# An mLSTM with a Fourier mixing block on one Trainium2 core: the second batch folded twice with named PSUM banks, a weight piece and the later recurrences moved by three slots

## The chip, the core and the metric

The kernel runs on one core of a Trainium2 chip. A core has a matrix engine (PE, with its weight loads listed apart as PEld), a vector engine (DVE), an activation engine (ACT), a general engine (POOL) and a queue that issues transfers (SP). Each runs its own instructions strictly in the order in which they were written; semaphores make one wait for another. SBUF is the working memory of all of them; PE writes its results to PSUM, which is divided into banks, and the others read them there. The metric is the time of one execution in microseconds (us), less being better. The time before is the median of three runs.

## What is computed

All of it is float32; the two weights arrive as float64 and are converted on the chip. First an mLSTM cell runs over 768 steps for 4 batches of 8 heads of width 40; its output, 768 rows of 320 per batch, goes through a Fourier mixing block with a normalization and a two-layer MLP of hidden width 1280:

```python
# mLSTM, per batch and head, for t in range(768):
m_new = np.maximum(f_gate[:, :, t] + m, i_gate[:, :, t])
f_stab = np.exp(f_gate[:, :, t] + m - m_new)
i_stab = np.exp(i_gate[:, :, t] - m_new)
C = f_stab * C + i_stab * outer(vt, kt)
n = f_stab * n + i_stab * kt
y[:, :, t] = sigmoid(o_gate[:, :, t]) * (C @ qt) / np.maximum(np.abs(n @ qt), 1.0)
...
# fnet block on x of (4, 768, 320)
mixed = np.real(np.fft.fft(np.fft.fft(x, axis=1), axis=2))
u = x + mixed
un = (u - mean(u)) / np.sqrt(var(u) + 1e-06)
out = u + np.maximum(un @ w_ch1, 0.0) @ w_ch2
```

## The kernel before

**Tiles and stages.** A batch has six chunks of 128 rows. The code counts batches from 0, so "batch 2" of the change's title is `b == 1`; below they are called by their index. Each batch runs through four stages:

- the recurrence, chunk by chunk and in halves of 64 rows (helper at L547): `ps` holds scores and the state's products, `ph` the outputs, `C0` to `C2` the state; `mlstm_mask`, `halves_decay` on POOL, `halves_add` (L703) and `halves_weigh` (L708) on DVE. `mlstm_finish` (L741 to L759) divides and multiplies by the gate, and writes the chunk into `x`;
- folding and the Fourier transform over rows: `mix_fold` (L828 to L846) adds and subtracts mirrored chunks and columns into `fe`; `mix_seq` and `mix_tail` multiply `fe` with the table `ds_sb` into `pz`, `pz` and `pzt`. For batches 2 and 3 `mix_fold_again` (L860, L862) first folds once more, and `mix_products_again` (L903) then needs narrower products than `mix_products` (L912 to L915), which batches 0 and 1 use;
- the transform over columns: `mix_feat` (L946) gives `pu`, one for each pair of chunks; `mix_add` (L968 to L974) adds each chunk's part of it to `x` on DVE and takes the row statistics; `mix_center` subtracts the mean on ACT into `uc`; `mix_turn` (L989) transposes `uc` on PE into `put`; `mix_turn_out` (L994) copies that to `uT` on ACT. For the middle pair (chunks 1 and 4) two short DVE instructions, L963 and L964, stand ahead of chunk 4's additions;
- the MLP: `pm` (L1058, L1067, L1129, L1134), relu into the hidden tiles, `po` (L1192 in `mlp_out` for batch 0, L1248 in `mlp_out_pair` for the others, which also need sums of hidden tiles on DVE, L1234), `residual` (L1198) and a store.

Chunks of these stages are taken in the order 0, 5, 1, 4, 2, 3 (`ORDER`).

**What sets the order.** The whole program is a plan written out by hand. `at(slot, phase, fn, ...)` puts a call into a slot (0 to about 150) and a phase in it; `run` goes through the plan in sorted order and issues every call there and then. The phases are `EVAC, FILL, MAIN, FILL_PE = range(4)`, with fractions between them. So a slot number is a place in the order, not a time, and each engine gets its instructions in this one order. In most slots `MAIN` is one step of some batch's MLP on PE, while another batch's recurrence and mixing are fitted in around it. In the profiled execution slot 51 begins at 117.75 us, slot 63 at 171.4, slot 83 at 209.9, slot 95 at 259.9 and slot 115 at 298.6.

**Batches beside each other.** `plan_batch(b, s_mlstm, s_mix, s_mlp)` starts the recurrence, the mixing and the MLP of a batch. The mixing and the last recurrence of batch 1 fall into the output stage of batch 0's MLP (slots 51 to 62: twelve half blocks of five `po` matmuls each, half by half for six blocks of rows); the recurrence of batch 2 begins in the same slots.

**Banks.** `bank(name, shape, n)` (L93) gives a PSUM tile in one of four banks, `pm0` to `pm3`. With a number it takes that bank; without one the next digit of a long string, `turn`. A tile that takes a bank waits until whatever was last in the bank has been read. Batches 2 and 3 take the numbers from the table `MIX` (L819): `pu` in banks 3, 2, 2 and `put` in 3, 3, 3, 3, 2, 3; batches 0 and 1 take them from the string.

**Weights.** Ten pieces are loaded as float64 and converted: `take` (L436, L438, DVE), `convert` (ACT), `join` (L450, L452, L456, DVE). Their slots are in the list `when`. The last piece, number 9, is the last part of the second weight.

Of the kernel before, what the change touches and what calls it, by code (L numbers as in the profile page):

```python
# [19 lines left out]
L = 128  # L20
# [37 lines left out]
def kernel(  # L58
# [723 lines left out]
    def plan_halves(b, s0, stride=3):  # L782
        at(s0 - 2, FILL + 0.7, halves_start, b)
        for c in range(NT):
            s = s0 + stride * c
            end = c == NT - 1
            t = 22 + 2 * c if b == 1 and c < 3 else s - 6
            at(t, FILL, mlstm_load, b, c)
            at(t, FILL, mlstm_load_max, b, c)
            at(t + 1 if c < 2 or b > 1 else s - 5, FILL, mlstm_load_decay, b, c)  # L790
            at(s - 2, FILL, mlstm_load_o, b, c)
            at(s - 2, FILL + 0.1, mlstm_scale_q, b, c)
            at(s - 2, FILL + 0.15, halves_alone, b, c)
            at(s - 1, FILL, mlstm_scale_v, b, c)
            at(s - 1, FILL, mlstm_exp, b, c, 0)
            at(s - 1, FILL + 0.5, mlstm_exp, b, c, NP)
            at(s, FILL, mlstm_mask, b, c)
            at(s, FILL_PE + 2.05, halves_scores, b, c)
            at(s, FILL_PE + 2.5, halves_to_state, b, c)
            for i in range(2):  # L800
                at(s + i, FILL + 0.05, halves_decay, b, c, i)
                at(s + 1 + i, FILL - 0.2, halves_add, b, c, i)
            at(s + 1, FILL, halves_weigh, b, c)
            at(s + 3, MAIN - 0.1 if end else FILL_PE, halves_from_state, b, c)
            at(s + 3, MAIN if end else FILL_PE + 0.5, halves_between, b, c)
            at(s + 3, FILL_PE + 3, halves_from_chunk, b, c)
            at(s + 3, FILL_PE + 0.6, mlstm_tanh, b, c)
            at(s + 4 + int((b, c) in ((2, 2), (3, 1))), FILL + 0.05, mlstm_finish, b, c)

# [4 lines left out]

    mixes = {}

    MIX = {"z": (2, 3), "zt": 2, "u": (3, 2, 2), "ut": (3, 3, 3, 3, 2, 3)}  # L819

    def copy(eng, out, in_):
        (nc.scalar.copy if eng == 0 else nc.vector.tensor_copy)(out=out, in_=in_)
# [41 lines left out]
    def mix_seq(b, p, parts):  # L864


        k = mixes.setdefault(b, Mix())
        if p == TG - 1:
            k.pz = getattr(k, "pz", []) + [bank("pz", [L, NK], MIX["z"][i] if b > 1 else None) for i in parts]
        for i in parts:  # L870
            if b < 2:
                mix_products(p, k.pz[i], i, slice(0, L))
            else:
                for product in mix_products_again(k, k.pz[i], i, slice(0, L)):
                    product()

    def mix_tail(b, p):

        k = mixes[b]
        if p == TG - 1:  # L880
            k.pzt = bank("pzt", [L, NK], MIX["zt"] if b > 1 else None)
        halves = [k.pzt[i * 64:(i + 1) * 64] for i in range(2)]
        if b < 2:
            for i in range(2):
                mix_products(p, halves[i], i, slice(L, PAD))
        else:

            a, z = (mix_products_again(k, halves[i], i, slice(L, PAD)) for i in range(2))
            for product in (a[0], z[0], a[1], z[1], a[2], z[2], a[3]):
                product()  # L890
# [37 lines left out]
    def mix_feat(b, p):  # L928

        k = mixes[b]
        m = slice(COL[p], COL[p] + L)
        pu = k.pu[p] = bank("pu", [L, DM + 1 + NC], MIX["u"][p] if b > 1 else None)
        if b == 0:
            products = ((pu[:, 0:DM + 1], k.Z[:, 0, m], dd_sb[:, 0]), (pu[:, 0:DM + 1], k.Z[:, 1, m], dd_sb[:, 1]),
                        (pu[:, 0:DM + 1], k.Zt[:, m], dd_sb[:, 2]))
        else:
            products = ((pu[:, 0:NC], k.Z[:, 0, m], dd_sb[:, 0, 0:NC]), (pu[:, NC:DM], k.Z[:, 1, m], dd_sb[:, 1, 1:HALF_D]),  # L940
                        (pu[:, 0:DM], k.Zt[:, m], dd_sb[:, 3, 0:DM]))
        if p == TG - 2:
            last, own = slice(LAST, LAST + 1), pu[0:1, DM + 1:]
            products += ((own, k.Z[:, 0, last], dd_sb[:, 0, 0:NC]), (own, k.Zt[:, last], dd_sb[:, 3, 0:NC]))
        for i, (o, z, t) in enumerate(products):
            nc.tensor.matmul(o, z, t, start=(i == 0), stop=(i in (2, 4)), skip_group_check=True)  # L946
# [37 lines left out]
    def mix_turn(b, c):  # L984

        k = mixes[b]
        pt = k.pt[c] = bank("put", [L, 3, L], MIX["ut"][ORDER.index(c)] if b > 1 else None)
        for ch in range(3):
            nc.tensor.transpose(pt[:, ch, :], k.uc[c].rearrange("p two n -> p (two n)")[:, ch * L:(ch + 1) * L], ident)  # L989

# [27 lines left out]
    def plan_mix(b, s0, x_done, s_feat, s_add, s_turn):  # L1018
        for j in range(TG):
            p = TG - 1 - j  # L1020
            at(x_done[j] + (b > 1 and j == TG - 1), FILL + 0.5 if b < 2 else FILL_PE + 0.2, mix_fold, b, p)
            if b == 0:
                at((s0 - 4, s0 - 2, s0)[j], FILL_PE + 4, mix_seq, b, p, (0, 1))
                at((s0 - 2, s0 - 2, s0)[j], FILL_PE + 4, mix_tail, b, p)
            elif b == 1 or j == 0:
                if b > 1:
                    for step, slot in enumerate((x_done[-1] + 2, x_done[-1] + 6)):
                        at(slot, FILL_PE + 0.25, mix_fold_again, b, step)
                at(s0, FILL_PE + 4, mix_seq, b, p, (0,))
                at(s0 + 1, FILL_PE + 4, mix_seq, b, p, (1,))  # L1030
                at(s0 + 2, FILL_PE + 4, mix_tail, b, p)
# [153 lines left out]
        nc.scalar.activation(out=h, in_=h, func=AF.Relu, scale=-1.0)  # L1185

    def mlp_out(b, gr, i, half):
        k = mixes[b]
        if half == 0:
            k.po = bank("po", [L, DM])  # L1190
        for f in range(half * NFF // 2, (half + 1) * NFF // 2):
            nc.tensor.matmul(k.po, hidden(gr, f)[:, i * L:(i + 1) * L], w2_sb[:, f, :], start=(f == 0), stop=(f == NFF - 1))  # L1192

    def residual(b, c, cols, po):

# [6 lines left out]

    def mlp_store(b, gr, i):
        c = ORDER[gr * TG + i]
        residual(b, c, slice(0, DM), mixes[b].po)
        store(b, c)


# [70 lines left out]
    def plan_mlp(b, s):  # L1279
# [27 lines left out]
        for gr in groups if b == 0 else ():  # L1307
            for i in range(TG):
                for half in range(2):
                    at(s, MAIN, mlp_out, b, gr, i, half)  # L1310
                    s += 1
                at(s, EVAC, mlp_store, b, gr, i)

    ctx.enter_context(tc.manual_schedule())
    eo_p = pool("eo", 1)
# [31 lines left out]
    s_mlp = 31  # L1347
    plan_batch(0, 0, 22, s_mlp)
    plan_batch(1, 32, 54, s_mlp + MLP_SLOTS)
    plan_batch(2, 51, 83, s_mlp + 2 * MLP_SLOTS)  # L1350
    plan_batch(3, 83, 115, s_mlp + 3 * MLP_SLOTS)
    for n in range(4):
        at(s_mlp + 2 * NFF + 1 + n, FILL + 0.4, weight_sums, n)
        at((56, 57, 58, 75)[n], FILL + 0.4, out_weight_sums, n)

    when = [((2, 0.7), (4, 0.5), (6, 0.6)), ((6, 0.7), (7, 0.5), (8, 0.6)), ((11, 0.7), (13, 0.5), (22, 0.6))]
    when += [((22, 0.7), (23, 0.7), (27, 0.6)), ((27, 0.7), (28, 0.7), (32, 0.6))]
    when += [((33, 0.7), (35, 0.7), (36, 0.6))] + [((s, 0.7), (s + 1, 0.7), (s + 2, 0.6)) for s in (36, 39, 42, 45)]
    pieces = w1_pieces + w2_pieces
    for n, (w, p) in enumerate(zip(when, pieces)):  # L1360
        if n > 4:
# [155 lines left out]
```

## Time and profile before

| | before |
|---|---|
| time, median of 3 runs | 404.14 us (402.89 to 404.44) |
| the profiled execution | 404.67 us |
| its span, first to last instruction | 402.9 us |
| mean granted clock of PE | 0.991 |
| PE busy | 387.8 us, 96% of the span |
| DVE busy | 279.8 us, 69% |
| ACT busy | 178.5 us, 44% |
| POOL busy | 128.0 us, 32% |

The span is what the trace covers; the profiled execution's time holds 1.8 us more. Two rows of the page show the span in 40 slices of 10.07 us, one digit per slice: PE's busy share in tenths, and the clock that was granted to PE in tenths of full speed:

```
PE   8999999999969999999999998999999999999996
PEclk9999999999989999999999999999999999999999
```

A 9 is 90% or more. The slice from 110.8 us has a 6 in the first row and an 8 in the second, the slice from 80.6 us an 8 in the second, and the slice from 241.8 us an 8 in the first; the first and the last slice hold the start and the end. The lines with the most idle time ahead of them on PE, from the page's costliest groups (line, engine, operation, out<-in with shapes, count | busy us, mean ns of one | idle before, and what ended most of it):

```
L1248 PE MATMUL po<-T,S 128*128 128x160 f32 x180 | 28.1, 303 | 2.6 <-DVE x L1198 2.6
L1129 PE MATMUL pm<-uT,w_sb 128*128 128x384 f32 x90 | 37.8, 507 | 0.2 <-DVE uT L1117 0.2
```

A float32 matmul is recorded as two instructions in the trace; five `po` matmuls of 128x320 appear as ten records and take 2.69 us when nothing interrupts them. Matmul ends are modelled, so a group's last row can overlap the next one's start by some tenths.

### The profile page before, as it was taken

Reading aid. Unit: us, or ns where it says so; the run is one execution under the profiler, and the core shown is the slowest. Engines: PE = TensorE matmul, PEld = TensorE weight load, DVE = VectorE, ACT = ScalarE, POOL = GpSimd, SP = SyncE. Lnnn points to the kernel's source line nnn. Section 1 sums busy time; section 2 is a strip of 40 time slices with the busy share of each in tenths; the row PEclk is TensorE's granted clock in tenths of the full one; section 3 lists DMA queues with packets and bytes.
Section 4 is the critical chain, followed back from the end, with each engine's and each line's share of the span. In section 5 each row is a group of like instructions: output and inputs, shape, how many; then the busy total and the mean of one; then the engine's idle time right before and its main releaser. Section 6 shows DMA issues by size and latency. Waiting matters only on the chain.

```text
span 402.9 us, 10837 instructions
## 1 busy us (share of the span) xinstructions
PE 387.8 (96%) x4324; PEld 283.3 (70%) x4324; DVE 279.8 (69%) x668; ACT 178.5 (44%) x513; POOL 128.0 (32%) x231
## 2 busy tenths in 40 slices
PE   8999999999969999999999998999999999999996
PEld 6887555556546776856569887855579997556996
DVE  7789976898867519787665689777663795336652
ACT  6898867576530213553562214544440023454000
POOL 5744425466945412261145304351200000020000
PEclk9999999989989999999999999999999999999999
DMA  7979499677752424365100525300000000000000
GB/s 197 278 227 320 121 240 257 194 242 240 191 151 70 142 87 131 109 196 150 54 26 2 157 82 170 103 20 2 1 0 18 17 34 33 2 0 0 34 34 34
DMA packets 22766, 43.96 MB, mean 109 GB/s; under 512 B 3492, under 2 KB 11388, under 8 KB 22588
## 3 DMA queue, kind: packets, MB, share of 16 engines
q1 hardware_dynamic: 22716, 43.27, 36.0%
q8 instruction: 34, 0.56, 0.5%
q14 instruction: 16, 0.13, 0.1%
HBM read 39.16 MB, written 4.10 MB: 107 GB/s over the span
## 4 chain that ended last, share of the span: by engine, by line
PE 80%; DVE 13%; issue 2%; POOL 2%; ACT 2%; DMA 0%; DVEq 0%; SPq 0%; POOLq 0%; ACTq 0%
PE po L1248 20%; PE pm L1129 16%; PE po L1192 8%; PE pm L1134 6%; PE ph L547 5%; PE ps L547 4%; PE pu L946 4%; PE pm L1067 4%; PE put L989 2%; PE pz L903 1%; PE pz L915 1%; DVE so L756 1%; PE pM L230 1%; PE pm L1058 1%; DVE x L759 1%
## 5 line engine op out<-in xcount | busy, mean ns | idle before, releaser
L1138 DVE TENSOR_TENSOR h<-h,pm 128x384 f32<-128x384 f32 x60 | 30.7, 550 | 30.6 <-PE pm L1129 16.5
L1198 DVE SCALAR_TENSOR_TENSOR x<-po,rstd,x 128x160 f32<-128x160 f32 (+1 forms) x69 | 27.0, 394 | 35.0 <-PE po L1248 32.3
L1129 PE MATMUL pm<-uT,w_sb 128*128 128x384 f32 x90 | 37.8, 507 | 0.2 <-DVE uT L1117 0.2
L543 POOL TENSOR_SCALAR_AFFINE_SELECT W<-W 64x512 f32<-64x512 f32 x36 | 27.9, 775 | 31.5 <-ACT W L518 30.4
L696 POOL TENSOR_TENSOR C<-C,decB 128x164 f32<-128x164 f32 x33 | 17.4, 528 | 62.1 <-DVE C L703 58.4
L518 ACT ACTIVATE W<-W,colT 128x64 f32<-128x64 f32 x144 | 36.5, 338 | 0.0
L1192 PE MATMUL po<-w_sb,h 128*128 128x320 f32 x120 | 35.2, 444 | 0.0
L1013 POOL TENSOR_TENSOR t<-rstd 128x6 f32<-128x6 f32 x12 | 2.6, 216 | 90.1 <-DVE v L1007 89.7
L1248 PE MATMUL po<-T,S 128*128 128x160 f32 x180 | 28.1, 303 | 2.6 <-DVE x L1198 2.6
L528 POOL TENSOR_TENSOR qg<-qk,Gb 128x512 f32<-128x512 f32 x21 | 27.3, 1298 | 9.5 <-DMA Gb<-G_d 9.5
L1192 PEld LDWEIGHTS po<-w_sb,h 128*128 128x128 f32 x120 | 22.7, 194 | 10.0 <-issue 1.5
L1067 PE MATMUL pm<-uT,w_sb 128*128 128x384 f32 x80 | 29.5, 505 | 0.1
L1248 PEld LDWEIGHTS po<-T,S 128*128 128x128 f32 x180 | 25.3, 190 | 4.5 <-DVE x L1198 3.4
L1248 PE MATMUL po<-w_sb,h 128*128 128x160 f32 x180 | 26.3, 300 | 0.0
L1248 PEld LDWEIGHTS po<-w_sb,h 128*128 128x128 f32 x180 | 25.2, 190 | 1.5 <-DVE x L1198 0.3
L994 ACT COPY uT<-put 128x384 f32<-128x384 f32 x24 | 11.1, 478 | 32.7 <-PE put L989 32.6
L1134 PE MATMUL pm<-uT,w1t_sb 64*128 64x384 f32 x120 | 25.2, 510 | 0.2 <-DVE h L1138 0.2
L1129 PEld LDWEIGHTS pm<-uT,w_sb 128*128 128x128 f32 x90 | 15.4, 189 | 14.0 <-DVE h L1138 4.9
L1185 ACT ACTIVATE h<-h 128x384 f32<-128x384 f32 x45 | 23.1, 520 | 2.0 <-DVE h L1138 2.0
L982 ACT ACTIVATE uc<-x 128x384 f32<-128x384 f32 x24 | 14.5, 614 | 18.9 <-DVE x L974 18.9
L703 DVE TENSOR_TENSOR C<-C,ps 128x164 f32<-128x164 f32 x33 | 10.5, 317 | 16.2 <-PE ps L547 13.6
L1067 PEld LDWEIGHTS pm<-uT,w_sb 128*128 128x128 f32 x80 | 14.5, 194 | 9.7 <-issue 1.4
(240 smaller groups left out, 860.8 us busy)
## 6 DMA issues: line engine op xcount, KB each, us to landing
kvt<-in_kv SPq DMA_DIRECT2D x24, 336.0 KB
qk<-in_qkT SPq DMA_DIRECT2D x48, 160.0 KB
raw<-in_w SPq DMA_DIRECT2D x10, 640.0 KB
Gb<-G_d SPq DMA_DIRECT2D x42, 128.0 KB
W<-M_d SPq DMA_DIRECT2D x36, 128.0 KB
so<-in_o SPq DMA_DIRECT2D x24, 160.0 KB
out<-x SPq DMA_DIRECT2D x24, 160.0 KB
ds_sb<-in_dft_s SPq DMA_DIRECT2D x1, 1158.0 KB
```

What stands on the lines that cost most here:

```text
L518: nc.scalar.activation(out=k.W[:, h, :], in_=M, func=AF.Exp, scale=-1.0, bias=colT[:, c, 0, b * H + h:b * H + h + 1])
L528: nc.gpsimd.tensor_tensor(out=k.qg[:, :, t], in0=k.qk[:, 0, :, t], in1=k.Gb[:, :, t], op=OP.mult)
L543: nc.gpsimd.affine_select(out=W, in_=W, compare_op=OP.is_ge, fill=0.0, base=base, pattern=[[0, H], [-1 if back else 1, LH]], channel_multi ...
L547: nc.tensor.matmul(out, w, x, start=start, stop=True, skip_group_check=True)
L1067: nc.tensor.matmul(k.pm[i], w1_sb[:, ch, f0:f0 + L], u[2 * ch], start=(ch == 0 and not ahead), stop=(ch == 1 and ahead), skip_group_check= ...
L1129: nc.tensor.matmul(bank, w, u, start=start, stop=True, skip_group_check=True)
L1134: nc.tensor.matmul(bank, block(w1t_sb, i)[rows], mlp_u(gr, 1)[rows], start=False, stop=True, skip_group_check=True)
L1138: nc.vector.tensor_tensor(out=h, in0=h, in1=bank, op=OP.add)
L1185: nc.scalar.activation(out=h, in_=h, func=AF.Relu, scale=-1.0)
L1192: nc.tensor.matmul(k.po, hidden(gr, f)[:, i * L:(i + 1) * L], w2_sb[:, f, :], start=(f == 0), stop=(f == NFF - 1))
L1198: nc.vector.scalar_tensor_tensor(out=u, in0=po, scalar=k.rstd[:, c:c + 1], in1=u, op0=OP.mult, op1=OP.add)
L1248: nc.tensor.matmul(po, a[:, f], w[:, f], start=start and f == 0, stop=f == half - 1, skip_group_check=True)
```

## The change

It makes these edits:

- Batch 1 is folded twice as batches 2 and 3 are: `mix_seq` and `mix_tail` take `mix_products_again` for every `b > 0`, and both steps of `mix_fold_again` are placed in the slot of its last fold. For batches 2 and 3 the second step comes four slots after the last fold instead of six.
- `pz`, `pzt`, `pu` and `put` of batch 1 get named banks. New entries of `MIX`, `u1` and `ut1`, hold those of `pu` and `put`: 3, 2, 3 and 2, 3, 2, 3, 2, 3. The output tiles `po` of batch 0 alternate between banks 0 and 1. The string `turn` is left as it was, and fewer tiles take from it.
- Piece 9 of the weights is taken, converted and joined in slots 48, 49 and 50 instead of 45, 46 and 47.
- The first two output blocks of batch 0 (`gr == 0`, `i` 0 and 1) run side by side: two hidden tiles of the one, two of the other, and so on over four half blocks, and the last two of the second block at the end. The store of the first then comes in the fourth of these slots.
- The recurrence of batch 2 starts in slot 54 instead of 51, that of batch 3 in 86 instead of 83. Everything in them moves along: loads, exponentials, masks, matmuls, finishes.
- `mlstm_finish` of batches 2 and 3 moves to phase `MAIN + 0.4` of its slot, and no chunk's comes a slot later any more.

```diff
--- before.py
+++ after.py
@@ -805,7 +805,7 @@
             at(s + 3, MAIN if end else FILL_PE + 0.5, halves_between, b, c)
             at(s + 3, FILL_PE + 3, halves_from_chunk, b, c)
             at(s + 3, FILL_PE + 0.6, mlstm_tanh, b, c)
-            at(s + 4 + int((b, c) in ((2, 2), (3, 1))), FILL + 0.05, mlstm_finish, b, c)
+            at(s + 4, FILL + 0.05 if b == 1 else MAIN + 0.4, mlstm_finish, b, c)
 
 
 
@@ -816,7 +816,7 @@
 
     mixes = {}
 
-    MIX = {"z": (2, 3), "zt": 2, "u": (3, 2, 2), "ut": (3, 3, 3, 3, 2, 3)}
+    MIX = {"z": (2, 3), "zt": 2, "u": (3, 2, 2), "ut": (3, 3, 3, 3, 2, 3), "u1": (3, 2, 3), "ut1": (2, 3, 2, 3, 2, 3)}
 
     def copy(eng, out, in_):
         (nc.scalar.copy if eng == 0 else nc.vector.tensor_copy)(out=out, in_=in_)
@@ -866,9 +866,9 @@
 
         k = mixes.setdefault(b, Mix())
         if p == TG - 1:
-            k.pz = getattr(k, "pz", []) + [bank("pz", [L, NK], MIX["z"][i] if b > 1 else None) for i in parts]
+            k.pz = getattr(k, "pz", []) + [bank("pz", [L, NK], MIX["z"][i] if b > 0 else None) for i in parts]
         for i in parts:
-            if b < 2:
+            if b == 0:
                 mix_products(p, k.pz[i], i, slice(0, L))
             else:
                 for product in mix_products_again(k, k.pz[i], i, slice(0, L)):
@@ -878,9 +878,9 @@
 
         k = mixes[b]
         if p == TG - 1:
-            k.pzt = bank("pzt", [L, NK], MIX["zt"] if b > 1 else None)
+            k.pzt = bank("pzt", [L, NK], MIX["zt"] if b > 0 else None)
         halves = [k.pzt[i * 64:(i + 1) * 64] for i in range(2)]
-        if b < 2:
+        if b == 0:
             for i in range(2):
                 mix_products(p, halves[i], i, slice(L, PAD))
         else:
@@ -932,7 +932,7 @@
 
         k = mixes[b]
         m = slice(COL[p], COL[p] + L)
-        pu = k.pu[p] = bank("pu", [L, DM + 1 + NC], MIX["u"][p] if b > 1 else None)
+        pu = k.pu[p] = bank("pu", [L, DM + 1 + NC], MIX["u" if b > 1 else "u1"][p] if b > 0 else None)
         if b == 0:
             products = ((pu[:, 0:DM + 1], k.Z[:, 0, m], dd_sb[:, 0]), (pu[:, 0:DM + 1], k.Z[:, 1, m], dd_sb[:, 1]),
                         (pu[:, 0:DM + 1], k.Zt[:, m], dd_sb[:, 2]))
@@ -984,7 +984,7 @@
     def mix_turn(b, c):
 
         k = mixes[b]
-        pt = k.pt[c] = bank("put", [L, 3, L], MIX["ut"][ORDER.index(c)] if b > 1 else None)
+        pt = k.pt[c] = bank("put", [L, 3, L], MIX["ut" if b > 1 else "ut1"][ORDER.index(c)] if b > 0 else None)
         for ch in range(3):
             nc.tensor.transpose(pt[:, ch, :], k.uc[c].rearrange("p two n -> p (two n)")[:, ch * L:(ch + 1) * L], ident)
 
@@ -1022,10 +1022,10 @@
             if b == 0:
                 at((s0 - 4, s0 - 2, s0)[j], FILL_PE + 4, mix_seq, b, p, (0, 1))
                 at((s0 - 2, s0 - 2, s0)[j], FILL_PE + 4, mix_tail, b, p)
-            elif b == 1 or j == 0:
-                if b > 1:
-                    for step, slot in enumerate((x_done[-1] + 2, x_done[-1] + 6)):
-                        at(slot, FILL_PE + 0.25, mix_fold_again, b, step)
+            elif j == 0:
+                for step in range(2):
+                    at(*((x_done[-1], FILL + 0.55) if b == 1 else (x_done[-1] + 2 + 2 * step, FILL_PE + 0.25)),
+                       mix_fold_again, b, step)
                 at(s0, FILL_PE + 4, mix_seq, b, p, (0,))
                 at(s0 + 1, FILL_PE + 4, mix_seq, b, p, (1,))
                 at(s0 + 2, FILL_PE + 4, mix_tail, b, p)
@@ -1185,11 +1185,20 @@
         nc.scalar.activation(out=h, in_=h, func=AF.Relu, scale=-1.0)
 
     def mlp_out(b, gr, i, half):
+
         k = mixes[b]
-        if half == 0:
-            k.po = bank("po", [L, DM])
-        for f in range(half * NFF // 2, (half + 1) * NFF // 2):
-            nc.tensor.matmul(k.po, hidden(gr, f)[:, i * L:(i + 1) * L], w2_sb[:, f, :], start=(f == 0), stop=(f == NFF - 1))
+        pair = gr == 0 and i < 2
+        if half == 0 and not (pair and i):
+            k.po = {n: bank("po", [L, DM], n % 2) for n in ((0, 1) if pair else (gr * TG + i,))}
+        blocks = ((i, range(half * NFF // 2, (half + 1) * NFF // 2)),)
+        if pair and i == 0:
+            blocks = [(n, range(f, f + 2)) for f in ((0, 2) if half == 0 else (4,)) for n in range(2)]
+        elif pair:
+            blocks = ((0, range(6, 8)), (1, range(6, 8)), (0, range(8, NFF))) if half == 0 else ((1, range(8, NFF)),)
+        for n, fs in blocks:
+            for f in fs:
+                nc.tensor.matmul(k.po[gr * TG + n], hidden(gr, f)[:, n * L:(n + 1) * L], w2_sb[:, f, :], start=(f == 0),
+                                 stop=(f == NFF - 1))
 
     def residual(b, c, cols, po):
 
@@ -1202,7 +1211,7 @@
 
     def mlp_store(b, gr, i):
         c = ORDER[gr * TG + i]
-        residual(b, c, slice(0, DM), mixes[b].po)
+        residual(b, c, slice(0, DM), mixes[b].po[gr * TG + i])
         store(b, c)
 
 
@@ -1309,7 +1318,10 @@
                 for half in range(2):
                     at(s, MAIN, mlp_out, b, gr, i, half)
                     s += 1
-                at(s, EVAC, mlp_store, b, gr, i)
+                if (gr, i) != (0, 0):
+                    at(s, EVAC, mlp_store, b, gr, i)
+                if (gr, i) == (0, 1):
+                    at(s - 1, MAIN - 0.1, mlp_store, b, 0, 0)
 
     ctx.enter_context(tc.manual_schedule())
     eo_p = pool("eo", 1)
@@ -1347,15 +1359,15 @@
     s_mlp = 31
     plan_batch(0, 0, 22, s_mlp)
     plan_batch(1, 32, 54, s_mlp + MLP_SLOTS)
-    plan_batch(2, 51, 83, s_mlp + 2 * MLP_SLOTS)
-    plan_batch(3, 83, 115, s_mlp + 3 * MLP_SLOTS)
+    plan_batch(2, 54, 83, s_mlp + 2 * MLP_SLOTS)
+    plan_batch(3, 86, 115, s_mlp + 3 * MLP_SLOTS)
     for n in range(4):
         at(s_mlp + 2 * NFF + 1 + n, FILL + 0.4, weight_sums, n)
         at((56, 57, 58, 75)[n], FILL + 0.4, out_weight_sums, n)
 
     when = [((2, 0.7), (4, 0.5), (6, 0.6)), ((6, 0.7), (7, 0.5), (8, 0.6)), ((11, 0.7), (13, 0.5), (22, 0.6))]
     when += [((22, 0.7), (23, 0.7), (27, 0.6)), ((27, 0.7), (28, 0.7), (32, 0.6))]
-    when += [((33, 0.7), (35, 0.7), (36, 0.6))] + [((s, 0.7), (s + 1, 0.7), (s + 2, 0.6)) for s in (36, 39, 42, 45)]
+    when += [((33, 0.7), (35, 0.7), (36, 0.6))] + [((s, 0.7), (s + 1, 0.7), (s + 2, 0.6)) for s in (36, 39, 42, 48)]
     pieces = w1_pieces + w2_pieces
     for n, (w, p) in enumerate(zip(when, pieces)):
         if n > 4:
```

## The prediction

> **What bounds the kernel now.** I read the page first: busy time, then the chain of waits, then the timelines of PE and DVE around every idle stretch of PE above 0.12 us, and last the busy time and granted clock of chosen windows. The chain's shares by engine:
>
> ```profile
> PE 80%; DVE 13%; issue 2%; POOL 2%; ACT 2%; DMA 0%; DVEq 0%; SPq 0%; POOLq 0%; ACTq 0%
> ```
>
> PE is busy for 387.8 of 402.9 us. So a change pays if it takes work from PE, closes one of its gaps, or keeps its clock up. All PE gaps over 0.12 us add up to 11.8 us; the four largest of those that end on DVE are 3.08 (at 110.98), 1.85 (248.01), 1.00 (80.54) and 0.75 us (235.63). The largest, in the timeline of PE and then of DVE (start, duration, engine, line, operation; in brackets the idle time before it and what ended it):
>
> ```profile
> 108.56 2.42 PE L1067 MATMUL pm<-uT,w_sb 128*128 128x384 f32 x7
> 114.06 0.68 PE L547 MATMUL ph<-C,qg 40*64 40x41 f32 x32 [3.08 <-DVE x L759]
> ...
> 117.68 1.91 PE L1192 MATMUL po<-w_sb,h 128*128 128x320 f32 x3
> ```
>
> ```profile
> 107.43 1.30 DVE L450 SCALAR_TENSOR_TENSOR e<-raw,e 128x640 uint32<-128x640 uint32 x1
> 108.65 1.08 DVE L452 SCALAR_TENSOR_TENSOR m<-raw,m 128x640 f32<-128x640 uint32 x1
> 109.77 1.77 DVE L456 TENSOR_TENSOR w_sb<-m,e 128x640 f32<-128x640 f32 x1
> ...
> 113.52 0.49 DVE L759 TENSOR_TENSOR x<-ph,so 128x320 f32<-128x320 f32 x1
> ```
>
> PE waits for the finish of the last but one chunk of batch index 1 (L759), and DVE is late with it because it converts the last piece of the second weight from 107.43 to 111.47. The windows (length, busy time and count of PE, PEld, DVE, ACT, POOL, clock, DMA share, GB/s) show what such gaps cost beyond themselves:
>
> ```profile
> 80.50:81.60 1.10, 0.10 (x6) 0.06 (x4) 1.10 (x3) 1.07 (x2) 0.42 (x1) 1.00 0.89 326
> 81.60:85.30 3.70, 3.70 (x101) 3.32 (x102) 3.60 (x8) 1.92 (x6) 1.80 (x3) 0.54 0.75 228
> 111.00:114.10 3.10, 0.04 (x4) 0.04 (x4) 2.86 (x9) 0.47 (x2) 0.00 (x0) 1.00 0.63 175
> 116.00:119.40 3.40, 3.40 (x39) 2.12 (x36) 1.30 (x5) 2.65 (x10) 3.09 (x9) 0.50 0.21 68
> ```
>
> After the gaps of 1.00 and of 3.08 us, and nowhere else, PE was granted half clock for about 3.4 us. In the second such stretch L1058 took 1.15 us instead of 0.85, ph 1.02 instead of 0.61 and the first ten records of po 3.73 instead of 2.69: 1.75 us lost.
>
> **What the change removes.**
>
> 1. The 3.08 us gap. Piece 9 of the weights is taken, converted and joined at slots 48, 49, 50 instead of 45, 46, 47, so its 4 us of DVE (L450, L452, L456) no longer stand ahead of that finish. What may be left is the path PE, ph, DVE, PE; I take 0.3 us left (0 to 0.7): -2.8. The piece is still in time: its join would end near 117, and the first matmul that reads its last columns now comes some 5 us later, behind the first blocks side by side. Without that margin the cost is the join's own 1.8 us.
> 2. The half clock behind it: -1.75.
> 3. Batch index 1 folds twice. PE spent 2.09 us (132.63 to 134.72), 1.94 (137.41 to 139.35) and 2.14 (142.14 to 144.28) on pz, pz, pzt; the same three in batch index 3, which is folded again already, took 1.38 (301.14 to 302.52), 1.33 and 1.52. 6.17 - 4.23 = -1.94. The two new DVE instructions (L860 0.55, L862 0.55 to 0.82) must end before the first pz; I place their end at 122.5 to 125 and PE's arrival near 126, so hidden; if late, up to 1.4.
> 4. Recurrences of batch indices 2 and 3 start at slots 54 and 86 instead of 51 and 83, with all that they issue: SP loads, ACT exponentials, POOL scales and masks, PE and DVE pieces. No queue loses or gains work. Their finishes also run at the end of slot s+4 instead of its middle (and no longer a slot later for two of them), and the second instruction of folding again comes two slots earlier after the last finish; both are single DVE groups of 1.7 and 0.6 us in slots where DVE has idle time, and cost nothing while that is so. It takes away one visible wait, DVE 1.87 us for the landing of a store, which delayed the residual that PE needed 4 us later:
>
> ```profile
> 231.24 0.49 DVE L759 TENSOR_TENSOR x<-ph,so 128x320 f32<-128x320 f32 x1 [1.87 <-DMA out<-x]
> ```
>
> ```profile
> 236.39 1.63 PE L1248 MATMUL po<-T,S 128*128 128x160 f32 x10 [0.75 <-DVE x L1198]
> 249.86 1.35 PE L1248 MATMUL po<-T,S 128*128 128x160 f32 x8 [1.85 <-DVE x L1198]
> ```
>
>  The 0.75 goes. The 1.85 stays nearly whole: in the new order L1234's two sums (1.65 and 1.35) and a finish still stand ahead of the residual, one finish slightly earlier. I take -1.0 for both (0 to -2.6).
>
> Side by side, blocks 0 and 1 of the output issue the same 20 matmuls; that costs nothing while the residual of block 0 (0.5 us of DVE) has five slots' room.
>
> **What it adds.** In batch index 1, pu and put now have named banks: pu in 3, 2, 3 and put in 2, 3, 2, 3, 2, 3. The first put (chunk 0) takes the bank of the second pu, the next one (chunk 5) that of the third pu. In the built order of before the first put waits on a read of the first pu, done long before; in the new one it must wait for L971 of chunk 4, and the next for L971 of chunk 3. PE and DVE there, before:
>
> ```profile
> 150.16 0.70 PE L946 MATMUL pu<-dd_sb,Zt 128*128 128x320 f32 x2
> 150.70 2.85 PE L1192 MATMUL po<-w_sb,h 128*128 128x320 f32 x10
> ...
> 158.00 0.49 PE L989 MATMUL put<-ident,uc 128*128 128x128 f32 x3
> ...
> 163.65 0.70 PE L946 MATMUL pu<-dd_sb,Zt 128*128 128x320 f32 x2
> 164.19 0.82 PE L989 MATMUL put<-ident,uc 128*128 128x128 f32 x6
> ```
>
> ```profile
> 150.90 0.33 DVE L968 TENSOR_TENSOR x<-x,pu 128x161 f32<-128x161 f32 x1 [1.33 <-PE pu L946]
> ...
> 161.06 0.31 DVE L971 TENSOR_TENSOR x<-x,pu 128x159 f32<-128x159 f32 x1
> ...
> 164.39 0.33 DVE L968 TENSOR_TENSOR x<-x,pu 128x161 f32<-128x161 f32 x1 [1.33 <-PE pu L946]
> ...
> 166.73 0.32 DVE L971 TENSOR_TENSOR x<-x,pu 128x159 f32<-128x159 f32 x1
> ```
>
> 5. First put. The first pu ends at 150.86 and PE reaches the put at 158.00, 7.14 us later. DVE, without idle, is at L971 of chunk 4 until 161.37, 10.47 us after it began on that pu at 150.90. The new order has the same kinds of rows between: the additions of chunks 0, 5, 1 and 4 (some 1.66 each with their statistics, the last 1.0 up to its L971), L963 and L964, weigh, finish, a residual, the 128x800 sum and L703. 10.5 - 7.1 = +3.4 (2.5 to 4). Behind the put on PE stand the matmuls of po and all else, so it is a gap of PE whole.
> 6. Second put, directly behind the third pu, which ended at 164.35; L971 of chunk 3 ended at 167.05: +2.7 (2.2 to 3).
> 7. The first pm of the MLP of this batch takes the bank of the last put and waits for ACT's copy out of it (L994; 0.48 alone, 0.84 for two): +0.7 (0.3 to 0.9).
> 8. Half clock behind 5 and 6. By the rows, gaps of 1.00 (among the small recurrence matmuls) and 3.08 us were followed by it, and 1.85 us among dense po was not. 3.4 and 2.7 lie on the side of 3.08. Full price is 1.75 us; where part of the half-clock stretch falls within the gap itself less. I take 1.5 each: +3.0 (0 to 3.5).
>
> [...]
>
> **Sum.** Removed: 2.8 + 1.75 + 1.94 + 1.0 = 7.5. Added: 3.4 + 2.7 + 0.7 = 6.8, and 3.0 of clock. Span 402.9 - 7.5 + 9.8 = 405.2. The profiled execution took 404.67 in all, 0.53 above the median; the difference of +2.3 is put on the median of 404.14: 406.4.
>
> **Rivals.** (What can be told from no change is 0.5%, 2.0 us: below 402.1, above 406.2.)
>
> - A, the forecast: both waits with half clock after both. 405 to 408, as the gaps come out at their low or high ends. Chance 0.42.
> - [...] 0.27.
> - C, faster: the recurrence of batch index 2 three slots later lightens DVE where the additions run, so that weigh and finish (0.57 + 1.70) fall behind L971 of chunk 4 and the first wait shrinks to 1.1, too short for half clock (-2.3 - 1.5); with both gaps near 236 and 248 gone (-1.6 more) the time is 406.4 - 5.4 = 401.0. Decides once the first wait is under 1.9. Against: the new order on DVE still has weigh and finish ahead. 0.16. That the change doesn't do what it says, the banks making no wait at all, would give 406.4 - 9.1 = 397; the waits are in the built program, so little of this chance.
> - D, slower than A: a new late piece downstream. The finishes of batch indices 2 and 3 come three slots nearer to their own folding. If DVE is behind there by the 1.9 us that it was at 231, pz waits as long and half clock follows: 1.9 + 1.75, in one batch 410, in both 413.7. Decides if the fold's last instruction ends later than PE's arrival at pz. Against: before, L862 of these two ended at 204.4 and 292.8, and pz began at 213.7 and 301.1, 9.3 and 8.3 us later; the new second fold is one slot later, some 2.5 us, which leaves 6. 0.15.
>
> **How the numbers follow.** Predicted is A, 406.4. Its own range is 405 to 408. With B whole, the upper part of C and the lower of D: 401.5 to 409.5. Two thirds of A and all of D lie above 406.2: slower 0.45; C below 402.1: 0.17; the rest, 0.38, within.
>
> **What would show it.** A gap of PE ahead of put at about 151.5 (158.0 less the 6.5 us of items 1 to 3) ended by DVE x L971, of 3.4 us; a second behind the third pu, of 2.7; clock rows of 0.5 after each; no gap at 111 and full clock at 116; pz groups of 1.4 us in batch index 1; no DVE wait for a store near 231. I am wrong if PE shows no wait for L971, if the gap near 111 has only moved to another wait (mask, decay or L703), or if gaps over 1 us appear after 180 where none was.

## The result, and the profile after

The changed kernel took 407.09 us (median of 9 runs, 405.8 to 408.4), the kernel before beside it 404.44 (9 runs): a ratio of 1.0068, 95% interval 1.0041 to 1.0095, so 0.7% slower. Measured once more (`e10_again`, 12 runs) the ratio was 1.0072 (1.0028 to 1.0116). The ratios and the comparisons at one clock, here and below, leave disturbed runs out, so a ratio is not always the quotient of the two medians.

The profiled execution has a span of 406.3 us against 402.9. Its page, busy PE and granted clock by slices of 10.16 us, and the chain by engines:

```profile
PE   8999999999999967899999998999999999999996
...
PEclk9999999999999988899999999999999999999999
...
PE 72%; DVE 18%; issue 3%; DMA 3%; POOL 2%; ACT 1%; DVEq 0%; SPq 0%; POOLq 0%; ACTq 0%
```

The 6 and the 8 in the slice from 110.8 us are gone. In their place stand 6, 7, 8 in three slices from 142 us, and three slices with lowered clock. In the chain of work that ended last, DVE's share rose from 13% to 18%. The timeline of PE at both places (start, duration, engine, line, operation; in brackets the idle time before and what ended it):

```profile
106.17 2.85 PE L1067 MATMUL pm<-uT,w_sb 128*128 128x384 f32 x8
108.94 0.68 PE L547 MATMUL ph<-C,qg 40*64 40x41 f32 x32
109.55 0.91 PE L1067 MATMUL pm<-uT,w_sb 128*128 128x384 f32 x2
...
111.84 11.03 PE L1200 MATMUL po<-w_sb,h 128*128 128x320 f32 x40
```

```profile
139.11 0.70 PE L946 MATMUL pu<-dd_sb,Zt 128*128 128x320 f32 x2
...
150.47 0.87 PE L989 MATMUL put<-ident,uc 128*128 128x128 f32 x3 [3.36 <-DVE x L971]
151.13 5.28 PE L1200 MATMUL po<-w_sb,h 128*128 128x320 f32 x10
...
162.88 1.51 PE L989 MATMUL put<-ident,uc 128*128 128x128 f32 x6 [2.83 <-DVE x L971]
164.18 3.90 PE L1200 MATMUL po<-w_sb,h 128*128 128x320 f32 x10
...
172.64 0.59 PE L1129 MATMUL pm<-uT,w_sb 128*128 128x384 f32 x1 [0.89 <-ACT uT L994]
```

`ph` of L547, which waited 3.08 us before, now follows without a gap, and forty `po` records run at full clock. Then come the three new waits of the prediction. Ten `po` records behind the first took 5.28 us instead of 2.86, behind the second 3.90. DVE in the same stretch, first and last row of the work that each put waits for:

```profile
139.85 0.32 DVE L968 TENSOR_TENSOR x<-x,pu 128x161 f32<-128x161 f32 x1 [1.33 <-PE pu L946]
...
150.01 0.32 DVE L971 TENSOR_TENSOR x<-x,pu 128x159 f32<-128x159 f32 x1
...
160.08 0.32 DVE L968 TENSOR_TENSOR x<-x,pu 128x161 f32<-128x161 f32 x1 [1.33 <-PE pu L946]
...
162.42 0.31 DVE L971 TENSOR_TENSOR x<-x,pu 128x159 f32<-128x159 f32 x1
```

From 139.85 to the end of chunk 4's L971 at 150.33 are 10.48 us, while PE needed 7.3 from the end of the first `pu` (139.81) to the put (147.11). Windows of the same trace (length; busy time and count of PE, PEld, DVE, ACT, POOL; clock; DMA share; GB/s):

```profile
147.20:149.20 2.00, 0.00 (x0) 0.00 (x0) 1.84 (x8) 0.00 (x0) 0.46 (x1) 1.00 0.52 158
149.20:150.40 1.20, 0.00 (x0) 0.00 (x0) 1.13 (x6) 0.00 (x0) 0.00 (x0) 0.50 0.88 297
150.40:153.80 3.40, 3.33 (x8) 2.38 (x9) 0.63 (x2) 1.50 (x3) 0.00 (x0) 0.50 0.15 48
153.80:156.00 2.20, 2.20 (x6) 1.35 (x4) 0.00 (x0) 0.00 (x0) 0.00 (x0) 0.50 0.00 0
160.10:162.80 2.70, 0.00 (x0) 0.00 (x0) 2.60 (x11) 0.00 (x0) 1.11 (x2) 1.00 0.64 216
162.90:166.30 3.40, 3.40 (x11) 2.63 (x12) 2.78 (x9) 1.47 (x3) 0.00 (x0) 0.50 0.20 72
```

PE idles while DVE is at work; half clock begins within the first gap, at 149.20, and lasts until 156.03, 6.83 us instead of the one stretch of about 3.4 that I had counted.

Where the time went can be read by taking the start of the same PE work in both traces and subtracting (before from after, us):

| first record of | difference | what changed since the row above |
|---|---|---|
| second put of batch index 0 | -0.8 | nothing that was edited; the start of the program |
| first pz of batch index 1 | -8.7 | gap at 111 gone, 3.1; half clock at 82 and at 116 gone, 3.0; 1.9 of recurrence not yet done |
| first pu of batch index 1 | -11.0 | fold, 1.8; 0.5 more of recurrence not yet done |
| matmuls of po behind the first put | -7.2 | wait 3.4; slow clock in the put 0.3, and 0.2 at its start, whose row no longer overlaps the one ahead |
| third pu | -4.3 | slow clock, 2.4; 0.5 of recurrence made up |
| put of chunk 4 | +0.4 | wait 2.8; slow clock 1.7, and 0.2 at the second put's start |
| first pz of batch index 2 | +3.6 | wait for L994 0.9; 1.2 at L1134; 0.8 of recurrence made up; rest 0.3 |
| first pz of batch index 3 | +3.4 | gaps near 236 and 248 smaller by 1.5; the rest of the recurrence, 1.1; rest 0.3 |
| last PE record | +3.4 | nothing |

The entries on the recurrence are what is left over, an estimate. The 1.2 at L1134 was not foreseen. DVE is behind there with the last weight sum, a normalization and a fold, and PE waits 0.38 us between the second and the third of eight records of half-height matmuls, and the eight took 2.78 us instead of 1.56 (the view ends ahead of the last). That is 0.8 more than the wait. In the profile before, the eight start in four pairs, the two of a pair 0.01 us apart (201.263 and 201.270 the first); in this one the two ahead of the break start 0.43 us apart (204.792 and 205.218) and the last two 0.32 (206.833 and 207.156), together 0.75:

```profile
204.79 0.91 PE L1134 MATMUL pm<-uT,w1t_sb 64*128 64x384 f32 x2
206.08 1.23 PE L1134 MATMUL pm<-uT,w1t_sb 64*128 64x384 f32 x5 [0.38 <-DVE h L1138]
```

### The profile page after: what moved, and what is told of

Its sections match the earlier page's. It is cut to its first block, busy times and chain, and to the rows that moved or that the text cites. A ratio compares the mean times of both kernels' runs of the same rounds, so it can differ in the third digit from the quotient of the medians.

```text
span 406.3 us, 10829 instructions
## 1 busy us (share of the span) xinstructions
PE 388.5 (96%) x4324; PEld 284.1 (70%) x4324; DVE 280.7 (69%) x670; ACT 178.7 (44%) x513; POOL 131.5 (32%) x231
## 4 chain that ended last, share of the span: by engine, by line
PE 72%; DVE 18%; issue 3%; DMA 3%; POOL 2%; ACT 1%; DVEq 0%; SPq 0%; POOLq 0%; ACTq 0%
PE po L1257 20%; PE pm L1129 13%; PE po L1200 7%; PE pm L1134 5%; PE pm L1067 4%; PE ph L547 4%; PE pu L946 3%; PE ps L547 3%; PE pz L903 2%; DMA raw<-in_w 2%; DVE so L756 2%; PE put L989 1%; DVE h L1138 1%; PE pm L1058 1%; PE pzt L903 1%
## 5 line engine op out<-in xcount | busy, mean ns | idle before, releaser
L1200 PE MATMUL po<-w_sb,h 128*128 128x320 f32 x120 | 37.5, 468 | 0.0
L1200 PEld LDWEIGHTS po<-w_sb,h 128*128 128x128 f32 x120 | 24.4, 208 | 10.5 <-issue 2.9
L528 POOL TENSOR_TENSOR qg<-qk,Gb 128x512 f32<-128x512 f32 x21 | 27.3, 1301 | 9.1 <-PE pu L946 9.1
L994 ACT COPY uT<-put 128x384 f32<-128x384 f32 x24 | 11.2, 477 | 39.5 <-PE put L989 39.3
L1134 PE MATMUL pm<-uT,w1t_sb 64*128 64x384 f32 x120 | 26.3, 511 | 0.4 <-DVE h L1138 0.4
L1257 PEld LDWEIGHTS po<-w_sb,h 128*128 128x128 f32 x180 | 25.2, 190 | 1.5 <-DVE x L1207 0.3
L1129 PEld LDWEIGHTS pm<-uT,w_sb 128*128 128x128 f32 x90 | 15.5, 189 | 14.8 <-DVE h L1138 5.9
L1134 PEld LDWEIGHTS pm<-uT,w1t_sb 64*128 64x128 f32 x120 | 12.8, 185 | 12.9 <-issue 8.2
```

The costliest lines, as they stand in the source:

```text
L528: nc.gpsimd.tensor_tensor(out=k.qg[:, :, t], in0=k.qk[:, 0, :, t], in1=k.Gb[:, :, t], op=OP.mult)
L1129: nc.tensor.matmul(bank, w, u, start=start, stop=True, skip_group_check=True)
L1134: nc.tensor.matmul(bank, block(w1t_sb, i)[rows], mlp_u(gr, 1)[rows], start=False, stop=True, skip_group_check=True)
L1200: nc.tensor.matmul(k.po[gr * TG + n], hidden(gr, f)[:, n * L:(n + 1) * L], w2_sb[:, f, :], start=(f == 0), stop=(f == NFF - 1))
L1257: nc.tensor.matmul(po, a[:, f], w[:, f], start=start and f == 0, stop=f == half - 1, skip_group_check=True)
```

## The experiments

Medians in us, each beside the kernel before on the same chip.

| run | this | before | ratio (95%) |
|---|---|---|---|
| e1_string | 395.99 | 404.6 | 0.9791 (0.9764 to 0.9818) |
| e2_first_put | 400.74 | 404.6 | 0.9901 (0.9875 to 0.9927) |
| e3_piece | 400.88 | 404.6 | 0.9907 (0.9885 to 0.9929) |
| e4_fold | 415.24 | 404.6 | 1.0261 (1.0233 to 1.0290) |
| e5_fold_once | 404.05 | 404.5 | 0.9965 (0.9921 to 1.0009) |
| e6_later | 402.13 | 404.5 | 0.9941 (0.9907 to 0.9974) |
| e7_in_turn | 396.06 | 404.5 | 0.9776 (0.9733 to 0.9819) |
| e8_piece_later | 398.62 | 404.5 | 0.9832 (0.9787 to 0.9878) |
| e10_again | 407.24 | 404.86 | 1.0072 (1.0028 to 1.0116) |
| e11_other_banks | 396.94 | 404.86 | 0.9856 (0.9814 to 0.9898) |
| e9_two_more | 396.72 | 404.86 | 0.9857 (0.9802 to 0.9912) |
| e12_sum_earlier | 395.17 | 405.09 | 0.9765 (0.9722 to 0.9808) |

### Do the named banks make the waits?

`e1_string`: the changed kernel, the five names of batch index 1 and `po` taken away.

```diff
-bank("pz", [L, NK], MIX["z"][i] if b > 0 else None)
+bank("pz", [L, NK], MIX["z"][i] if b > 1 else None)
...
-bank("put", [L, 3, L], MIX["ut" if b > 1 else "ut1"][ORDER.index(c)] if b > 0 else None)
+bank("put", [L, 3, L], MIX["ut"][ORDER.index(c)] if b > 1 else None)
...
-bank("po", [L, DM], n % 2)
+bank("po", [L, DM])
```

> The changed kernel, with pz, pzt, pu and put of batch index 1 and po of batch index 0 in banks from the string again; everything else as changed. Theory (the named banks make PE wait for L971 twice and for L994 once, with half clock behind the first two): the three gaps of 3.4, 2.8 and 0.9 us and the two stretches of half clock (some 2.75 and 1.7 us lost) go, so 11.5 us less than the changed kernel: about 395.5, against 404.4 for the kernel before. Rival (the waits come from DVE being late with the additions there, because the second fold brings PE to them earlier; any banks would wait): the gaps stay at over 2 us and the time is 403 or more.

Measured: 395.99. PE's timeline shows both places without a wait:

```profile
148.72 0.49 PE L989 MATMUL put<-ident,uc 128*128 128x128 f32 x3
149.04 2.86 PE L1200 MATMUL po<-w_sb,h 128*128 128x320 f32 x10
...
155.36 0.82 PE L989 MATMUL put<-ident,uc 128*128 128x128 f32 x6
156.01 2.86 PE L1200 MATMUL po<-w_sb,h 128*128 128x320 f32 x10
```

With the same fold, pieces and slots, and DVE doing the same additions, the gaps are gone and `po` takes 2.86 us again. The banks alone cost some 11 us, and the rest of the change is worth 2.1%.

`e2_first_put`: one number.

```diff
-"ut1": (2, 3, 2, 3, 2, 3)
+"ut1": (3, 3, 2, 3, 2, 3)
```

> The changed kernel, with the bank of the first put (chunk 0) of batch index 1 changed from 2 to 3, the one of the first pu. Theory: the first gap (3.4) and the half clock behind it (2.75) go, the second gap (2.8) and the third (0.9) stay: about 401. Rival (the two waits are one lateness of DVE: what is not waited for at the first put is waited for at the second): the second gap grows by the first to some 6 us, and the time is within 2 us of the changed kernel's 407.

Measured: 400.74. The first put runs through, the second waits as long as before; the two are separate waits, not one lateness:

```profile
148.61 0.49 PE L989 MATMUL put<-ident,uc 128*128 128x128 f32 x3
...
158.25 0.84 PE L989 MATMUL put<-ident,uc 128*128 128x128 f32 x6 [2.83 <-DVE x L971]
...
166.35 1.56 PE L1129 MATMUL pm<-uT,w_sb 128*128 128x384 f32 x4 [0.88 <-ACT uT L994]
```

`e11_other_banks`: is it naming, or these numbers?

```diff
-"ut1": (2, 3, 2, 3, 2, 3)
+"ut1": (3, 2, 0, 2, 0, 2)
```

> The changed kernel with all its named banks, but with put of batch index 1 in banks 3, 2, 0, 2, 0, 2 instead of 2, 3, 2, 3, 2, 3, so that no put takes a bank whose pu is still being read. Theory (not naming, but these six numbers cost the time): the gaps of 3.4, 2.8 and 0.9 us go, 395.3 to 396.7, as with banks from the string. Rival (fixed banks for po or pu cost too): a gap of over 0.5 us stays between 138 and 172, and 397 or more.

Measured: 396.94, a little above the stated band; its runs without any lowered clock lay at 396.85 to 397.0. Of the three gaps there is left

```profile
161.57 0.91 PE L1129 MATMUL pm<-uT,w_sb 128*128 128x384 f32 x2 [0.24 <-ACT uT L994]
```

and the profile has a gap of 0.6 us at 244.7 that ends on nothing visible. It is not the names': `e9_two_more`, with banks from the string and on the same chip, has it too (0.54), and so has `e10_again` (0.60). At full clock the spans are 395.1 to 395.3 us against 393.8 to 394.3 for `e1_string`, some 1.0 more, and 0.6 of that is this gap, 0.2 the wait for L994. So six numbers made the loss; names as such cost at most some tenths.

### What are the other parts worth alone?

`e3_piece`: the kernel before with `(36, 39, 42, 48)` in place of `(36, 39, 42, 45)`.

> The kernel before, with only the last weight piece three slots later. Theory: the gap of 3.1 us at 111 and the half clock behind it (1.7) go and nothing takes their place, as the join ends more than 2 us ahead of the first matmul that reads it: about 399.6. Rival (without the two output blocks side by side the piece is late): PE waits up to 2 us for L456 in the first output block, and half clock follows: 402 to 404.

Measured: 400.88, between the two theories. PE does not wait for L456. The gap shrank to 0.81 and a new one came behind it:

```profile
110.03 0.68 PE L547 MATMUL ph<-C,qg 40*64 40x41 f32 x32 [0.81 <-DVE x L759]
...
113.96 0.68 PE L547 MATMUL ph<-kvt,W 64*64 64x41 f32 x32 [1.56 <-ACT warm L739]
```

```profile
110.41 0.83 ACT L443 ACTIVATE e<-e,ebias 128x640 uint32<-128x640 uint32 x1 [2.60 <-DVE e L436]
111.15 0.72 ACT L444 ACTIVATE m<-m 128x640 f32<-128x640 uint32 x1
111.78 2.00 ACT L518 ACTIVATE W<-W,colT 128x64 f32<-128x64 f32 x8
113.68 0.13 ACT L739 COPY warm<-ph 1x1 f32<-1x1 f32 x1
```

ACT now has the piece's conversion and eight exponentials of the next batch ahead of the small copy L739 that PE waits for. The 0.81 ahead of it stands with DVE, where L756, the instruction before L759, took 1.54 us instead of the 0.49 of the changed kernel:

```profile
107.91 1.54 DVE L756 SCALAR_TENSOR_TENSOR so<-so,den 128x320 f32<-128x320 f32 x1
```

In this trace POOL's L528, which scales for the next batch's recurrence, runs beside it from 107.84 to 109.11; in the traces of the changed kernel and of `e8_piece_later` POOL is idle then and L756 takes 0.49. That the one slows the other is read from this and not tested by itself.

`e6_later`: the kernel before with only

```diff
-plan_batch(2, 51, 83, ...); plan_batch(3, 83, 115, ...)
+plan_batch(2, 54, 83, ...); plan_batch(3, 86, 115, ...)
...
-at(s + 4 + int((b, c) in ((2, 2), (3, 1))), FILL + 0.05, mlstm_finish, b, c)
+at(s + 4, FILL + 0.05 if b == 1 else MAIN + 0.4, mlstm_finish, b, c)
...
-enumerate((x_done[-1] + 2, x_done[-1] + 6))
+enumerate((x_done[-1] + 2, x_done[-1] + 4))
```

> The kernel before, with only the recurrences of batch indices 2 and 3 three slots later, their finishes at the end of the slot, and the second step of folding again two slots earlier. Theory as predicted (only the wait of DVE for a store and some of the gaps near 236 and 248 go; the gap at 111 stays, being the weight piece's): 403.1 to 404. Rival (with the recurrence of batch index 2 out of slots 45 to 53, DVE, ACT and POOL are freer there, so that the gap at 111 shrinks too): below 402.5, with a gap at 111 of under 2 us.

Measured: 402.13, the rival's time. The gap at 111, still ended by L759, shrank to 2.15 us, a little above the rival's bound, and in this profile no half clock followed it:

```profile
112.72 0.68 PE L547 MATMUL ph<-C,qg 40*64 40x41 f32 x32 [2.15 <-DVE x L759]
```

`e8_piece_later` has both edits:

> The kernel before, with the last weight piece and the recurrences later, without the second fold, the named banks and the blocks side by side. Theory (the 2.4 us of gaps that the piece alone still left near 109 to 114 go once the recurrence starts three slots later): no gap there, and about 397.9, which is 396.0 and 1.85 for the fold. Rival (what closed that gap in the changed kernel is the other edits): gaps of over 1.5 us stay there, about 400.

Measured: 398.62, and no gap over 0.3 us between 82 and 195:

```profile
109.19 0.68 PE L547 MATMUL ph<-C,qg 40*64 40x41 f32 x32
...
111.49 0.68 PE L547 MATMUL ph<-kvt,W 64*64 64x41 f32 x32
```

With the exponentials three slots later, the copy comes in time. Set against `e3_piece` in the two traces, the later recurrences take 3.5 us off PE's idle time (the largest parts are 2.4 here, 0.7 near 232, 0.8 near 244 and 0.2 at 263, less 0.4 for the new gap at 196), and cost 1.0 of PE time; the last record comes 2.5 us earlier.

`e4_fold` was meant to be the second fold alone, but the edit issued the fold and its products three times; its 415.24 says nothing on the question.

> The kernel before, with only the second fold of batch index 1, its tiles in banks from the string. Theory: PE has 1.8 to 1.9 us less to do and nothing waits for L862: about 402.5. Rival (the two added DVE instructions delay what PE waits for there, or DVE sets the pace of that stage anyway): within 0.7 us of 404.4.

`e5_fold_once` issues them once.

> The kernel before, with the second fold of batch index 1 and its products once each, tiles in banks from the string. Theory: PE has 1.85 us less to do (6.17 less 4.34) and nothing waits for L862: about 402.7 against 404.6. Rival (the added DVE instructions, some 1.3 us, delay work for which PE waits): within 0.7 us of 404.6.

Measured: 404.05, a ratio whose interval holds 1: the medians favour the rival, though not surely. The trace does not: from the first `pz` to the first `pu` of the batch PE needed 15.03 us (132.72 to 147.75) instead of 16.88 (132.63 to 149.51), and up to 213 us it stayed 1.8 ahead of the kernel before. Then half clock came, from 249.26 to 252.67, behind a gap of 1.86 us that in the kernel before had cost no clock. Runs with the same mean granted clock speak for the theory as well: at 0.991 the median is 403.1 us (3 runs) against 404.3 (7 runs of the kernel before on the same chip), at 0.986 and 0.987 it is 404.1 (5) against 405.7 (3). So the fold wins some 1.2 to 1.6 us there, most of what was counted, which the medians over all clocks hide.

`e7_in_turn`: `e1_string` with `mlp_out` and its store as before the change.

> The changed kernel with banks from the string (396.0), and with the first two output blocks one after the other again, the first block's store behind it. Theory (the last weight piece is joined over 2 us ahead of the first block's need either way): 395.3 to 396.7, no gap that ends on L456. Rival (side by side is what gives the late piece its time): a gap of PE of 1 us or more that ends on L456, and 397.5 or more.

Measured: 396.06, with no gap that ends on L456. The blocks side by side neither cost nor bring anything that these runs show.

### Does a better version exist?

Two of the remaining gaps were tried, on top of `e7_in_turn`.

```diff
-at((56, 57, 58, 75)[n], FILL + 0.4, out_weight_sums, n)
+at((56, 57, 58, 72)[n], FILL + 0.4, out_weight_sums, n)
...
-at(s + 4, FILL + 0.05 if b == 1 else MAIN + 0.4, mlstm_finish, b, c)
+at(s + 4 + int((b, c) == (3, 0)), FILL + 0.05 if b == 1 else MAIN + (0.6 if (b, c) == (3, 0) else 0.4), mlstm_finish, b, c)
```

> The changed kernel with banks from the string and the first blocks in turn, and two more moves: the last of the weight sums (L1220, 1.0 us of DVE) from slot 75 to 72, where DVE has 2.4 us idle, and the finish of chunk 0 of batch index 3 from slot 90 to the end of 91, behind the sums that PE waits for. Theory: the gap of 0.4 at 193 and the 0.9 that the split of L1134 costs behind it go, and the gap of 1.1 at 237: 2.4 off 396.0, about 393.7. Rival (what DVE does not do there it does a little later, ahead of the next thing that PE waits for): gaps of the same size further on, 395 or more.

Measured: 396.72. The gap at 193 went, but of the one at 237 there was 0.68 left, and the moved finish made another 0.79 at 241 (the gap at 244 named above, 0.54 here, comes on top):

```profile
237.24 1.63 PE L1248 MATMUL po<-T,S 128*128 128x160 f32 x10 [0.68 <-DVE x L1198]
241.01 0.68 PE L547 MATMUL ph<-C,qg 40*64 40x41 f32 x32 [0.79 <-DVE x L759]
```

So `e12_sum_earlier` keeps the first line of the diff alone.

> The changed kernel with banks from the string and the first blocks in turn (396.1), and only the last of the weight sums (L1220) moved from slot 75 to 72; the finish of chunk 0 of batch index 3 stays in slot 90. Theory (with the finish also moved, 0.9 us was won near 193 by this sum and given back near 237 to 241 by the finish): no gap at 193, the 1.1 at 237 as before, and 395.1. Rival (the two moves can't be told apart this way, the loss is the sum's): gaps of 0.7 us or more at 236 to 241 beside it, 396.5 or more.

Measured: 395.17, ratio 0.9765 (0.9722 to 0.9808): eight records of L1134 without a gap, the wait at 237 as it was. It has the lowest median of the study, 2.3% under the kernel before, though it can't be told apart from `e1_string` and `e7_in_turn` by its interval.

```profile
192.22 1.95 PE L1134 MATMUL pm<-uT,w1t_sb 64*128 64x384 f32 x8
...
236.82 1.62 PE L1248 MATMUL po<-T,S 128*128 128x160 f32 x10 [1.08 <-DVE x L1198]
```

### The clock, by itself

> The changed kernel once more, unaltered, for how its time goes with the number of half-clock stretches. Theory (its runs differ mainly in how many windows of 3.4 us are granted half clock, at 1.7 to 1.9 us each): spans rise by 3.5 to 4 us for each 0.0085 that the mean clock falls, and even its best clock leaves it above 400 us by the three gaps. Rival (the clock is the same in all runs and the spread has another cause): no such relation.

Measured: twelve runs from 402.88 to 410.24 us. At a mean clock of 0.999 they took 402.9 and 403.3, at 0.991 406.7 to 407.8, at 0.986 and 0.987 408.2 to 408.6, at 0.982 and 0.983 409.7 and 410.2. From 0.999 to 0.991 that is 3.6 us, as the theory has it. Its profile shows one stretch of half clock behind the first wait, which cost 1.4 us as its first 0.7 us fell into the wait, and none behind the second:

```profile
150.70:153.50 2.80, 2.76 (x7) 2.03 (x8) 0.61 (x2) 1.50 (x3) 0.00 (x0) 0.50 0.24 70
153.50:156.90 3.40, 3.40 (x113) 2.63 (x112) 0.55 (x1) 0.49 (x2) 0.00 (x0) 1.00 0.00 0
158.90:161.80 2.90, 0.06 (x2) 0.08 (x2) 2.74 (x11) 0.00 (x0) 1.19 (x2) 1.00 0.66 209
161.80:165.20 3.40, 3.40 (x17) 2.56 (x18) 2.76 (x9) 1.37 (x3) 0.00 (x0) 1.00 0.20 73
```

## Why the prediction was right

The median moved by +2.65 us, +2.3 was forecast, and the mechanism named as the likeliest is what the runs show: three waits for banks, larger than what the other edits won. By its items:

1. **Gap at 111, -2.8.** In the full change it went whole, -3.1. But the reason given was half of it: the piece alone left 2.4 us of gaps (`e3_piece`), the recurrences alone 2.15 (`e6_later`), and only both together left none (`e8_piece_later`). The step "its 4 us of DVE no longer stand ahead of that finish" overlooked ACT, which converts the same piece (1.56 of the 2.4), and L756 beside POOL (0.81).
2. **Half clock behind it, -1.75.** Gone, and in this execution the one at 82 as well, 3.0 for both; no edit touches that one, and the profiles of `e1_string` and `e2_first_put` have it again. That the one at 82 went was luck.
3. **Fold, -1.94.** 1.8 in the traces of the changed kernel and of `e5_fold_once`; L862 ended at 121.1, in time for the first pz at 123.9.
4. **Later recurrences, -1.0.** Mis-sized. The gaps near 236 and 248 shrank by 1.5 (the latter from 1.85 to 1.08), the gap at 111 owes its other half to them, and they brought the unforeseen 1.2 at L1134: the gap of 0.38 there is in `e6_later` and `e8_piece_later`, and not in `e3_piece`.
5. **First put, +3.4.** 3.36. PE came to it at 147.1 and not, as forecast, at 151.5: some 2.4 us of recurrence were still to be done, the half clock at 82 was missing, and the start was 0.8 earlier.
6. **Second put, +2.7.** 2.83.
7. **First pm, +0.7.** 0.89.
8. **Half clock behind both, +3.0.** 2.8 and 1.7 in the first profile, 1.4 and nothing in the second. The reason given, the length of the gap, was not enough: the second gap of 2.83 us was followed by half clock in the one and not in the other (on what differed, see the last section). Each half-clock stretch of 3.41 us takes 0.0042 off the mean clock of a run of 405 us, so by an estimate from their clocks the 21 runs of the changed kernel had from none (two runs) to four, and 15 of them two or three. The kernel before pays for half clock too: the mean of its clock over 62 runs is 0.989, that of the changed kernel over 21 runs 0.990. At equal clock the change costs 2.3 us (from 0.990 to 0.992 the median is 404.5 before, of 30 runs, and 406.8 after, of 8), so nearly all of the loss is waiting and work, and the clock term, with the one removed in item 2, came out even.

Blocks side by side at nothing was right (`e7_in_turn`). Rival B, half clock behind one wait or none, happened in single executions: in the profile of `e10_again` none followed the second gap, which was split on the grid of the last section. Rival C did not: the first wait was 3.36 in both profiles of the changed kernel. Rival D did not either: no `pz` waited. That the total came so near is in part luck: item 4, the clock at 82 and the earlier start, which were not counted, stand against item 8 in the profiled execution and L1134.

Two readings of the profile before were slightly off, and nothing rests on them: 11.8 us is the sum of all gaps of PE, those above 0.12 make 11.7; and the list of the largest gaps that end on DVE leaves out one of 1.24 us at the start of the program.

By length, the gaps of 3.08 (before), 3.26 (`e5_fold_once`) and 3.36 us (both profiles of the changed kernel) were each followed by half clock. Length alone did not decide, though: half clock also followed gaps of 0.91 us (`e1_string`, at 80), 1.86 us (`e5_fold_once`) and 2.83 us (the changed kernel), and did not follow one of 2.83 (`e2_first_put`).

## What to carry to other kernels

A buffer's number is an edge in the order of the program: giving a tile a bank makes the writing engine wait for the last reader of whatever was there (here 3.36, 2.83 and 0.89 us). So for each tile ask who reads its predecessor, where that reader stands in its own engine's queue, and what stands behind the writer; here six numbers turned a gain of 2% into a loss of 0.7%. And if a stall is removed, look at all engines that the moved work passes, because the next late one (here ACT) may leave most of it in place.

## What was not expected of the hardware

In the profiles before and after, half clock was granted in stretches of 3.41 us or of two of these end to end (only the one at the very end of the execution is shorter, 2.26 and 3.15), and within one execution they lie on one grid of that step. Before, it was granted from 81.87 to 85.28 and from 116.00 to 119.41, and 116.00 - 81.87 is ten times 3.41; in the changed kernel's profile from 149.20 to 156.03 and from 162.86 to 166.27, and 162.86 - 149.20 is four times 3.41. Counted back in these steps, the first step begins 3.36 us into the span before and 2.43 after, so the grid lies elsewhere in each of the two. In the traces here, where a gap lay on the grid counted for more than its length. In the changed kernel 2.82 us of the second gap fell into one step (159.45 to 162.86), and half clock followed, 1.7 us of PE time. In `e10_again`, the same kernel, the gap was split at 160.31 into 1.39 and 1.45, in `e2_first_put` at 156.75 into 1.33 and 1.50, and none followed. The gap of 1.85 us near 248 was split at 249.12 into 1.11 and 0.74 in the kernel before and cost no clock; in `e5_fold_once` the same gap (1.86) fell whole into one step and half clock came, from 249.26. Idle time is not all of it: near 81, among small matmuls, gaps of 0.9 to 1.0 us within one step were followed by half clock in some executions (before, `e1_string`) and not in others (the changed kernel, `e10_again`).

So the same kernel, in `e10_again`, lay anywhere in 7 us (402.88 to 410.24), in line with its mean clock (0.999 to 0.982). Comparing two kernels at the same mean clock told the second fold of `e5_fold_once` from none, where the medians did not.
